# The layout of the products in a banded attention's value stage

## The chip, the core and the metric

The kernel runs on one core of one Trainium2 chip. The metric is the device time of one execution in microseconds (us). The core has five engines that work side by side, each in the order of its own instruction stream: TensorE (PE, with its weight loads as PEld), VectorE (DVE), ScalarE (ACT), GpSimd (POOL) and SyncE (SP, which here only issues transfers). They meet through semaphores.

## What is computed

A sum of two attentions goes through a gated feed-forward part with an RMS norm ahead of it. The local attention sees, for every token, only the seven tokens at distance -3 to 3:

```python
q_d = q.reshape(B, H, Sd, factor, D).mean(axis=3)      # k_d, v_d alike; factor = 4
out_up = np.repeat(sm_attn(q_d, k_d, v_d), factor, axis=2)
mask = np.abs(pos[:, None] - pos[None, :]) < factor
scores = np.where(mask, scale * np.matmul(q, k.transpose(0, 1, 3, 2)), -1000000000.0)
out_local = np.matmul(softmax(scores), v)
x = (out_up + out_local), as rows of 8 heads x 64        # 4608 tokens x 512
xn = x / rms * rms_g
out = (silu(xn @ w_gate) * (xn @ w_val)) @ w_out         # inner width 1536
```

B = 8, H = 8, S = 576, D = 64. Everything is float32; the weights come as float64 bits.

## The kernel before

**Chunks.** The 4608 tokens are worked off in 18 chunks of 256. A chunk is made of two units (`j`) of 128 tokens. In a unit a partition stands for (segment of 36 tokens, batch, head pair), and along the partition lie parity (two heads), 4 tokens and 64 elements.

**The banded attention of a chunk** (class `Attention`) runs in eight steps `i`, one for each unit, parity and pair of tokens (`trio`). Each step has 2 tokens x 7 offsets x 64 elements = 896 numbers per partition:

- `score` (L427) multiplies q by the seven neighbours of k, `score_sum` (L433) adds up 64 elements for each of the 14 scores, both on DVE. Then comes a softmax over seven (L443 to L470).
- `value_scalar` (L480) and `value` (L489) write the seven products of a share and a row of v into a tile `prod`: the first `na` offsets on ACT, one instruction for each token and offset with 64 elements; the last two on POOL, one instruction of 256 elements; what lies between on DVE. `na` is 1 in chunk 0, 2 in chunks 1 and 2, 3 in chunk 3, and 4 from chunk 4 on, so DVE's share is 512, 384, 384, 256 and then 128 elements.
- `value_sum` adds up the seven products. In chunks 0 and 1 (`self.pt` set) PE does it with products by the identity (L504), from chunk 2 on DVE with one reduction (L509).

The tile `prod` has two buffers, which scores and values share: a step's products can only be written when the sum two steps back has read its own.

Behind the eight steps come the sum with the coarse attention (L526), squares on ACT (L532), the norm's mean on PE (L539), an inverse root (L547 and L554 on DVE, then from chunk 2 on three Newton steps on POOL, L564 to L567), the scaling (L571, DVE), the transposes on PE (L582) and the split of x into `xh` (L584, ACT) and `xl` (L588, DVE).

**The feed-forward part of a chunk** (class `Inner`) has 12 tiles `f` of the inner width. Each is 24 products of 256 columns on PE (L658), a tanh on ACT (L664), two DVE operations (L667, L672), a rounded copy `hs` on ACT (L677) and its rest (L680, on POOL in chunks 0 and 1, on DVE after them); two tiles later follow six products of 512 columns (L639). `ps_h`, in which the products of L658 land, has three buffers.

**The order.** In chunk `c` the loop at L1057 puts the attention steps of chunk `c + 1`, and up to four pairs of heads of the coarse attention (L292 to L361), between the tiles `f`, at places given by numbers in `steps` (L592). So the value steps of chunk `c + 1` share DVE and ACT with the feed-forward part of chunk `c`. Chunk 0, with the decoding of the weights, has an order worked out from rough times of instructions (L1019 to L1054). DVE, POOL and SP then keep program order. The coarse attention's sums of four tokens are made by transfers: SP issues a plain load (L279), POOL three that accumulate onto it (L277), each after the one before has landed. POOL has them in the same queue as the products (L489) and the Newton steps.

Of the kernel before, what the change touches and what calls it, by code (L numbers as in the profile page):

```python
# [8 lines left out]
FP32 = mybir.dt.float32  # L9
# [8 lines left out]
DRAM = bass.MemoryType.DRAM  # L18

P = 128  # L20
B, H, S, D = 8, 8, 576, 64
FAC = 4                 # tokens per group of the coarse attention; half-width of the band
SD = S // FAC           # 144 groups
HALF = SD // 2          # 72
NO = 2 * FAC - 1        # 7 diagonals
HALO = FAC - 1
SP = S + 2 * HALO
DM, DF = H * D, 1536
KT = DM // P            # 4 head pairs, also the contraction tiles of the first products
NF = DF // P            # 12  # L30
NPAIR = B // 2
SEG = 36                # tokens of a segment; partition = (segment 16, batch 2, head pair 4)
NSEG = S // SEG
US = 4                  # tokens of every segment in one unit of work
UPP = SEG // US         # units per pair of batches
NU = NPAIR * UPP        # 36 units of 128 tokens
C = 256                 # tokens of a chunk of the feed-forward part
NCH = NU // 2
WPC = 512               # weights decoded at a time, per partition
LAG = 2  # L40
# [52 lines left out]
def attn_moe_kernel(  # L93
# [21 lines left out]
    band = ctx.enter_context(tc.tile_pool(name="band", bufs=2))  # L115
# [13 lines left out]
    class Weight:  # L129
        """A weight's tiles, the last four in places that hold raw weights first."""  # L130

# [24 lines left out]

    # A float64 weight comes as its bits. Its high word, read as a float32, is scaled so that the top
    # of its exponent is float32's (what lies under float32's normal range goes towards zero); moved
    # up by three, and joined by the sign and the top three bits of the low word, it is the weight's
    # float32, which (times the norm's gain) is split exactly into two float32r parts.  # L160
    def load_weight(src, hi_lo, f, n, gain, k):
# [10 lines left out]

        # The sign and the last bits come in one word: the low one, or (signed zeros) the high one.
        def last_bits(engine):
# [63 lines left out]
        def split_on_tensor(pool, tag):  # L238
            # w * gain - hi as products with diagonals, exact but for the rounding of w * gain
            hi, lo = st["hi"], st["lo"]  # L240
            lp = pool.tile([P, *hi.shape[1:]], FP32, name=tag)
            nc.tensor.matmul(out=lp, lhsT=ident_sb if k is None else diag["gain"][:, k], rhs=st["w"], start=True, stop=False)
            nc.tensor.matmul(out=lp, lhsT=diag["minus"], rhs=hi, start=False, stop=True)
            nc.scalar.copy(out=lo, in_=lp)
# [15 lines left out]

# [1 line left out]
    up_dram = {}  # L262
# [23 lines left out]
    class Coarse:  # L286
        """Two heads of the coarse attention."""

# [88 lines left out]

# [1 line left out]
    def load_kv(src, u, par):  # L379
# [7 lines left out]

    def window(t, s0, o0=0, o1=NO):
        b_ = t[:, :, :]
# [11 lines left out]
    class Attention:  # L401
        """The banded attention, the sum with the coarse one, and the norm of one chunk's tokens."""

# [68 lines left out]
        def value_scalar(self, i):  # L472
            j, par, s0 = trio[i]
            if (j, par) not in self.v:
                self.load_value(j, par)
            pr = self.pr[i] = band.tile([P, NO, 2, D], FP32, name="prod")
            p = self.sc[:, j, par, s0:s0 + 2]
            for s in range(2):
                for o in range(self.na):
                    nc.scalar.activation(  # L480
                        out=pr[:, o, s], in_=self.v[j, par][:, s0 + s + o], func=AF.Copy, scale=p[:, s, o:o + 1],
                    )
# [144 lines left out]

# [1 line left out]
    late = []  # L629
# [18 lines left out]
    class Inner:  # L648
        """One tile of the feed-forward part's inner width."""

# [35 lines left out]

# [1 line left out]
    coarse = [(b, hp) for b in range(B) for hp in range(KT)]  # L688
    done = 2 * KT

    # The weights' decoding, the first two chunks' attention and the first chunk's feed-forward part
    # share VectorE, in an order worked out from rough times of the instructions.
    class Clock:
# [32 lines left out]
    finished, decoded, fetched, rank = {}, [], [], {}  # L726
# [28 lines left out]

    # TensorE's clock halves while it idles; products that nobody reads keep it up in the gaps.
    def warm_lane():
# [173 lines left out]
    def raw_loads():  # L931
        # Until they are written, the weights' last places hold raw ones.
        first = [(w, 1, h) for w in wg + wv for h in range(2)]
        second = [(w, i, 0) for w in wo for i in (1, 2)]
        users = {}
        for n, piece in enumerate(pieces):
            if n < place[0, 16]:
                options = [("first", i) for i in range(NF1)] + [("second", i) for i in range(NF2)]
            else:
                options = [("stage", i) for i in range(RAW_BUFS)]  # L940
                options += [("second", i) for i in range(4) if n < (place[1, NF - 4] if i % 2 == 0 else place[1, NF - 2])]

            def slot():
                free = [(finished[users[o]] if o in users else RAW_AT, o) for o in options if users.get(o) in finished or o not in users]
                return min(free) if free else None

            yield lambda: slot() and max(slot()[0], RAW_AT)
            kind, i = o = slot()[1]
            users[o] = "raw done", n
            spot = {"first": first, "second": second, "stage": [None] * RAW_BUFS}[kind][i]  # L950
            load(("raw", n), lambda: piece[0](spot and spot[0].raw_place(*spot[1:])), 1.46)
# [45 lines left out]
    scaled = {n for (t, _), n in place.items() if t == 0}  # L997
# [21 lines left out]
    with tc.manual_schedule(engines={mybir.EngineType.DVE, mybir.EngineType.Pool, mybir.EngineType.SP}):  # L1019
# [3 lines left out]
        group = [sum_loads(0, 0, nc.scalar)]  # L1023
# [33 lines left out]
    for c in range(1, NCH):  # L1057
        todo = []
        if c + 1 < NCH:
# [5 lines left out]
            for i, it in enumerate(coarse[done:done + n]):  # L1065
                at = 0.2 + 5.0 * i / n
# [3 lines left out]
        for f in range(NF):  # L1070
            it = Inner(att, f)
# [3 lines left out]
            while todo and todo[0][0] < f + 1:  # L1075
                step = todo.pop(0)[1]
# [12 lines left out]
def _layouts(i):  # L1089
    import numpy as np  # L1090
    q, k, v = i["q"], i["k"], i["v"]
    a = {}
    a["q_band"] = q.reshape(NPAIR, 2, KT, 2, NSEG, UPP, US, D).transpose(0, 5, 3, 4, 1, 2, 6, 7).reshape(NU, 2, P, -1)
    pad = ((0, 0), (0, 0), (HALO, HALO), (0, 0))
    a["k_pad"], a["v_pad"] = np.pad(k, pad), np.pad(v, pad)
    t = np.stack([q, k], 1).reshape(B, 2, 2, 2, 2, SD, FAC, D)  # batch, q/k, half, head pair, parity, group, j, d
    a["qk_sum"] = t.transpose(0, 6, 4, 7, 2, 1, 3, 5).reshape(B, FAC, P, 2, -1)
# [42 lines left out]
```

## Time and profile before

Three runs took 1214.41, 1214.95 and 1220.25 us; the median is 1214.95.

| | us |
|---|---|
| median of the runs | 1214.95 |
| span of the profiled execution | 1216.1 |
| its own time beside the span | not given by the page |
| DVE, sums of the value stage (L509), 128 | 224.1 |
| ACT, products of the value stage (L480), 1024 | 262.6 |
| POOL, products of the value stage (L489), 144 | 114.2 |
| chunks 12 to 15, from end to end | 54.6 each |
| chunk 17, without any attention beside it | 44.2 |

The span runs from the first to the last instruction. "Busy" is the time in which at least one instruction of the engine was under way. In a row of a group the numbers after the bar are busy time in us, mean duration of one in ns, and the idle time of the engine ahead of them with what ended it ("<-"). A name such as `prod<-sc,kv` says what is written from what. Matmuls are pipelined and their ends are modelled, so a PE without a gap isn't PE at its peak; the granted clock is a share of full speed. Here is the page's picture of the span in 40 slices (busy tenths):

```profile
PE   1894766998999999999999999999999999999998
DVE  5699997699979898888887979798898989898332
ACT  0467643446464747464637464747464654637221
POOL 3467675355131212121212121211112121211000
```

The first seven slices or so are the decoding of the weights and chunk 0, the last three have no attention left.

### The profile page before, as it was taken

How to read it: one execution, taken by the hardware profiler on the slowest of the kernel's cores; microseconds unless marked ns; L12 is line 12 of the kernel's file. 1: busy time of each engine (PE TensorE's matmuls, PEld its weight loads, DVE VectorE, ACT ScalarE, POOL GpSimd, SP SyncE). 2: the span in 40 equal slices, each digit the busy share in tenths (PEclk: the TensorE clock that was granted, in tenths of full speed). 3: DMA queues.
4: the chain of work that ended last, by engine and by line, in shares of the span. 5: the costliest groups of instructions: out<-in, count | busy, mean ns of one | idle time of the engine just before them, and what ended most of it. 6: DMA issues, size and time to landing. Idle time of an engine off the chain costs nothing. (4 is left out here: it accounts for less than half of the span.)

```text
span 1216.1 us, 22187 instructions
## 1 busy us (share of the span) xinstructions
PE 1104.6 (91%) x7944; PEld 1011.3 (83%) x7944; DVE 1012.4 (83%) x1766; ACT 617.1 (51%) x2241; POOL 339.3 (28%) x520
## 2 busy tenths in 40 slices
PE   1894766998999999999999999999999999999998
PEld 1674766988999998989898989899989898989997
DVE  5699997699979898888887979798898989898332
ACT  0467643446464747464637464747464654637221
POOL 3467675355131212121212121211112121211000
PEclk9565788998999999999999999999999999999999
DMA  9946538355536161616161616132222313120000
GB/s 242 227 140 200 194 90 197 96 131 95 139 70 149 34 151 42 150 42 147 41 144 44 148 43 148 43 99 61 72 79 59 85 53 90 48 85 18 1 19 18
DMA packets 77294, 119.57 MB, mean 98 GB/s; under 512 B 27264, under 2 KB 36736, under 8 KB 77184
## 3 DMA queue, kind: packets, MB, share of 16 engines
q1 hardware_dynamic: 47760, 91.12, 25.5%
q0 software_dynamic: 11520, 21.24, 11.4%
q10 hardware_dynamic: 17904, 5.80, 2.1%
q8 instruction: 62, 1.02, 0.4%
q14 instruction: 48, 0.39, 0.1%
HBM read 106.33 MB, written 11.80 MB: 97 GB/s over the span
## 5 line engine op out<-in xcount | busy, mean ns | idle before, releaser
L639 PE MATMUL ps_o<-wo,hs 128*128 128x512 f32 x1296 | 363.4, 401 | 20.7 <-DVE hs L680 18.4
L658 PE MATMUL ps_h<-xh,wg 128*128 128x256 f32 x1728 | 358.6, 286 | 8.6 <-DVE sil L672 8.6
L658 PE MATMUL ps_h<-xh,wv 128*128 128x256 f32 x1728 | 340.5, 279 | 0.0
L658 PEld LDWEIGHTS ps_h<-xh,wg 128*128 128x128 f32 x1728 | 288.9, 193 | 21.1 <-DVE sil L672 11.2
L480 ACT ACTIVATE prod<-kv,sc 128x64 f32<-128x64 f32 x1024 | 262.6, 338 | 50.8 <-DVE x_t L509 35.2
L658 PEld LDWEIGHTS ps_h<-xh,wv 128*128 128x128 f32 x1728 | 281.5, 189 | 3.2 <-issue 0.2
L639 PEld LDWEIGHTS ps_o<-wo,hs 128*128 128x128 f32 x1296 | 221.7, 189 | 58.0 <-DVE hs L680 22.6
L658 PE MATMUL ps_h<-xl,wg 128*128 128x256 f32 x864 | 247.5, 286 | 1.0 <-DVE xl L588 1.0
L658 PE MATMUL ps_h<-xl,wv 128*128 128x256 f32 x864 | 241.7, 280 | 0.0
L509 DVE TENSOR_REDUCE x_t<-prod 128x128 f32<-128x896 f32 x128 | 224.1, 1762 | 6.3 <-PE ps_a L582 3.4
L677 ACT ACTIVATE hs<-sil 128x256 fp32r<-128x256 f32 x216 | 89.8, 416 | 203.5 <-DVE sil L672 170.2
L489 POOL TENSOR_TENSOR prod<-sc,kv 128x256 f32<-128x256 f32 x144 | 114.2, 813 | 272.1 <-DVE x_t L509 116.5
L658 PEld LDWEIGHTS ps_h<-xl,wg 128*128 128x128 f32 x864 | 166.9, 193 | 8.8 <-DVE xl L588 1.2
L658 PEld LDWEIGHTS ps_h<-xl,wv 128*128 128x128 f32 x864 | 163.5, 189 | 1.6
L427 DVE TENSOR_TENSOR prod<-q_t,kv 128x896 f32<-128x896 f32 x140 | 152.4, 1090 | 10.0 <-DMA q_t<-in_q_band_dram 9.7
L664 ACT ACTIVATE sil<-ps_h 128x256 f32<-128x256 f32 x216 | 81.6, 378 | 150.0 <-PE ps_h L658 125.6
L433 DVE TENSOR_REDUCE sc<-prod 128x14 f32<-128x896 f32 x144 | 153.7, 1076 | 0.0
L667 DVE SCALAR_TENSOR_TENSOR sil<-sil,ps_h 128x256 f32<-128x256 f32 x216 | 89.4, 414 | 61.5 <-ACT sil L664 61.5
L680 DVE TENSOR_TENSOR hs<-sil,hs 128x256 fp32r<-128x256 f32 x192 | 80.3, 418 | 32.6 <-ACT hs L677 32.6
L277 POOL DMA_DIRECT2D qk<-in_qk_sum_dram x42 | 38.5, 916 | 190.9 <-DMA qk<-in_qk_sum_dram 172.6
L672 DVE SCALAR_TENSOR_TENSOR sil<-sil,ps_h 128x256 f32<-128x256 f32 x216 | 89.0, 412 | 2.1
L532 ACT ACTIVATE up_t<-x_t 128x128 f32<-128x128 f32 x144 | 44.1, 306 | 45.1 <-DVE x_t L526 43.0
(116 smaller groups left out, 1132.2 us busy)
## 6 DMA issues: line engine op xcount, KB each, us to landing
kv<-in_k_pad_dram SPq DMA_DIRECT2D x72, 320.0 KB
kv<-in_v_pad_dram SPq DMA_DIRECT2D x72, 320.0 KB
qk<-in_qk_sum_dram POOLq DMA_DIRECT2D x42, 288.0 KB, 4.7
out_dram<-o_sb SPq DMA_DIRECT2D x36, 256.0 KB
q_t<-in_q_band_dram SPq DMA_DIRECT2D x70, 128.0 KB
vs<-in_v_sum_dram POOLq DMA_DIRECT2D x42, 144.0 KB, 3.5
wg<-in_w_gate_dram SPq DMA_DIRECT2D x8, 512.0 KB
wg<-in_w_val_dram SPq DMA_DIRECT2D x8, 512.0 KB
```

The costliest lines, as they stand in the source:

```text
L427: engine.tensor_tensor(out=pr[:, :, a:b], in0=bcast(q[:, s0:s0 + 2], 2, b - a), in1=window(k, s0, a, b), op=ALU.mult,)
L433: nc.vector.tensor_reduce(out=self.sc[:, j, par, s0:s0 + 2], in_=self.pr[i], axis=AX.X, op=ALU.add,)
L480: nc.scalar.activation(out=pr[:, o, s], in_=self.v[j, par][:, s0 + s + o], func=AF.Copy, scale=p[:, s, o:o + 1],)
L489: engine.tensor_tensor(out=self.pr[i][:, a:b], in0=bcast(p[:, :, a:b].rearrange("p s o -> p o s"), 3, D), in1=window(self.v[j, par], s0, a ...
L509: nc.vector.tensor_reduce(out=self.x[j][:, s0:s0 + 2, par], in_=pr.rearrange("p o s d -> p s d o"), axis=AX.X, op=ALU.add,)
L639: nc.tensor.matmul(out=o_ps[c][j], lhsT=lhs[:, cols], rhs=rhs(f)[:, 0], start=(f == 0 and i == 0), stop=(f == NF - 1 and i == 2),)
L658: nc.tensor.matmul(out=hp_[:, t], lhsT=wi(f)[:, 0, k], rhs=xi[:, k], start=(n == 0), stop=(n == 3 * KT - 1),)
L664: nc.scalar.activation(out=self.sil, in_=hp_[:, 0], func=AF.Tanh, scale=0.5)
L667: nc.vector.scalar_tensor_tensor(out=self.sil, in0=self.sil, scalar=1.0, in1=self.p[:, 0], op0=ALU.add, op1=ALU.mult,)
L672: nc.vector.scalar_tensor_tensor(out=self.sil, in0=self.sil, scalar=0.5, in1=self.p[:, 1], op0=ALU.mult, op1=ALU.mult,)
L677: nc.scalar.activation(out=self.hh, in_=self.sil, func=AF.Copy)
L680: (nc.gpsimd if self.c in REST_P else nc.vector).tensor_tensor(out=self.hl, in0=self.sil, in1=self.hh, op=ALU.subtract,)
```

## The change

From chunk 2 on, where DVE does the sum, the tile `prod` is allocated in the order (token, element, offset) and not (offset, token, element). A rearranged view gives the rest of the program the axes it had. So the seven products of one output lie next to each other: the reduction reads 896 numbers without a step, where it stepped by 128 numbers (512 bytes), and every product is written with a step of 7 numbers (28 bytes), where it was written densely. That holds for all three writers, ACT (L480), DVE and POOL (L489). Chunks 0 and 1, whose sums PE makes, keep the old layout.

```diff
             if (j, par) not in self.v:
                 self.load_value(j, par)
-            pr = self.pr[i] = band.tile([P, NO, 2, D], FP32, name="prod")
+            pr = band.tile([P, NO, 2, D] if self.pt else [P, 2, D, NO], FP32, name="prod")
+            pr = self.pr[i] = pr if self.pt else pr.rearrange("p s d o -> p o s d")
             p = self.sc[:, j, par, s0:s0 + 2]
...
                 self.x[j][:, s0:s0 + 2, par], in_=pr.rearrange("p o s d -> p s d o"), axis=AX.X, op=ALU.add,
```

(The last line is not changed; it shows the view that the sum reads.) The rest of the diff takes out comments. No instruction is added, removed or moved: on every engine the same instructions stand in the same order and wait for the same engines. Lines behind L476 move down by one in the changed kernel; names with a line number here mean the kernel before, unless said otherwise.

## The prediction

> **What bounds the kernel now.** The first view is the page: its head,
>
> ```profile
> span 1216.1 us, 22187 instructions
> ```
>
> and its busy times (share of the span, instructions):
>
> ```profile
> PE 1104.6 (91%) x7944; PEld 1011.3 (83%) x7944; DVE 1012.4 (83%) x1766; ACT 617.1 (51%) x2241; POOL 339.3 (28%) x520
> ```
>
> TensorE (PE) is the bound on average, VectorE (DVE) next. An average says nothing of a stage, so the second view is the busy time by stretches, cut at ends of chunks over the part in which the changed sums run, 234 to 1122 us. Columns: stretch, length, busy time (instructions) of each engine, granted TensorE clock, DMA share, GB/s.
>
> ```profile
> 234.30:305.40 71.10, 66.09 (x486) 60.52 (x485) 68.72 (x108) 39.95 (x159) 36.08 (x49) 0.93 0.57 123
> 305.40:425.30 119.90, 118.98 (x896) 109.35 (x895) 108.68 (x197) 69.03 (x272) 28.64 (x53) 1.00 0.42 97
> 425.30:790.20 364.90, 351.41 (x2605) 321.27 (x2604) 310.71 (x573) 199.48 (x775) 78.97 (x156) 0.98 0.42 95
> 790.20:847.80 57.60, 57.60 (x436) 52.74 (x436) 52.03 (x96) 33.28 (x130) 8.05 (x20) 1.00 0.26 70
> 847.80:903.40 55.60, 54.54 (x418) 50.75 (x417) 50.76 (x91) 31.29 (x120) 8.59 (x20) 1.00 0.27 73
> 903.40:1121.90 218.50, 206.94 (x1482) 192.10 (x1482) 199.92 (x336) 117.65 (x438) 40.20 (x80) 1.00 0.23 65
> ```
>
> Length less PE's busy time is what PE stands still: 5.0, 0.9, 13.5, 0, 1.1 and 11.6 us, together **32 us**. To this comes what a lower granted clock costs: 7% of 71 us is 5.0 us, 2% of 365 us is 7.3 us. So however much DVE is relieved, some 44 us is the ceiling. The third view is PE's waits, asked for each stretch (us in total, times, longest), here from 234 to 305 us:
>
> ```profile
> PE ps_o L639 <- POOL hs L680: 2.3, 2, 1.8
> PE ps_a L304 <- DVE xl L588: 1.7, 1, 1.7
> PE ps_h L658 <- DVE xl L588: 1.0, 1, 1.0
> ```
>
> from 425 to 790 us:
>
> ```profile
> PE ps_o L639 <- DVE hs L680: 13.5, 8, 2.7
> ```
>
> and from 848 to 1122 us:
>
> ```profile
> PE ps_h L658 <- DVE sil L672: 7.7, 8, 1.7
> PE ps_o L639 <- DVE hs L680: 4.9, 5, 1.1
> ```
>
> Nearly always PE waits for a small DVE instruction. What matters is what stands ahead of that one on DVE, which works in program order. The change leaves the order on every engine as it was, so the rows of the timeline can be walked with new durations.
>
> **The sums (line 509).** From the groups of instructions, shapes kept apart (busy us, mean ns of one, idle before):
>
> ```profile
> L509 DVE TENSOR_REDUCE x_t<-prod 128x128 f32<-128x896 f32 x128 | 224.1, 1762 | 6.3 <-PE ps_a L582 3.4 <-ACT prod L480 2.5 <-issue 0.4
> L433 DVE TENSOR_REDUCE sc<-prod 128x14 f32<-128x896 f32 x144 | 153.7, 1076 | 0.0
> ...
> L452 DVE TENSOR_REDUCE m_b<-sc 128x16 f32<-128x112 f32 x18 | 4.6, 258 | 0.0
> ```
>
> The score sum (L433) reads as many elements, 896, without a step and takes 1076 ns; L509 reads them with a step of 512 bytes and takes 1762. New, it reads runs of seven and gives 128 results. Does a short run cost? L452 reads runs of seven: between it and L433 lie 784 elements and 818 ns, 1.04 ns each, at 16 and 14 results, so a run of seven shows no price. I take **1.08 us**, 0.69 us less; 128 sums make 88 us of DVE. Bounds: 1.08 (no such read is shown faster) and 1.76 (the step was not the cause).
>
> **The writes.** Each product now lands 28 bytes from the last. The writers in the same view, on ACT and on POOL:
>
> ```profile
> L480 ACT ACTIVATE prod<-kv,sc 128x64 f32<-128x64 f32 x1024 | 262.6, 338 | 50.8 <-DVE x_t L509 35.2 <-DVE sc L470 10.8 <-ACT xh L584 3.1
> ```
>
> ```profile
> L489 POOL TENSOR_TENSOR prod<-sc,kv 128x256 f32<-128x256 f32 x144 | 114.2, 813 | 272.1 <-DVE x_t L509 116.5 <-ACT xh L584 96.5 <-DVE m_g L317 27.1
> ```
>
> The nearest that the trace has, an ACT instruction with a dense output and one that writes every second word:
>
> ```profile
> L171 ACT ACTIVATE o_sb<-wg 128x512 f32<-128x512 f32 x24 | 15.9, 662 | 16.7 <-DMA wg<-in_w_gate_dram 7.1 <-DMA wg<-in_w_out_dram 2.7 <-POOL wg L232 2.7
> ```
>
> ```profile
> L179 ACT ACTIVATE wg<-wg 128x512 uint32<-128x512 uint16 x8 | 5.3, 666 | 0.5 <-DMA wg<-in_w_val_dram 0.5
> ```
>
> Of L480's 1024 writes 976 change (8 per sum from chunk 4 on, 4 and 6 in chunks 2 and 3; the first two chunks' 48 don't), and 128 writes each on POOL and DVE. No row shows such a write. From below: L179 writes every second word and takes 666 ns where L171, its output dense, takes 662; so nothing. A gain is excluded: the same elements lay in one run before. From above: the price of L509's step, 686 ns over 896 elements, 0.77 ns each: 0.05 us for an ACT write (64 elements), 0.10 for a DVE one (128), 0.20 for a POOL one (256). The nearest row is L179, so I take nothing for ACT and DVE; for POOL, already at 3.2 ns an element, half the upper end, 0.1 us.
>
> [...]
>
> **From 848 to 1122 us: 12.6 us idle.** Chunk 12's end in the timeline (start, length, [idle before]): PE,
>
> ```profile
> 954.32 0.73 PE L639 MATMUL ps_o<-wo,hs 128*128 128x512 f32 x2 [0.94 <-DVE hs L680]
> ...
> 961.34 0.39 PE L658 MATMUL ps_h<-xh,wg 128*128 128x256 f32 x1 [1.60 <-DVE sil L672]
> ```
>
> DVE,
>
> ```profile
> 939.21 3.48 DVE L509 TENSOR_REDUCE x_t<-prod 128x128 f32<-128x896 f32 x2 [0.53 <-PE ps_a L582]
> ...
> 959.29 1.67 DVE L509 TENSOR_REDUCE x_t<-prod 128x128 f32<-128x896 f32 x1
> 960.87 0.41 DVE L672 SCALAR_TENSOR_TENSOR sil<-sil,ps_h 128x256 f32<-128x256 f32 x1
> ```
>
> and ACT:
>
> ```profile
> 941.09 3.94 ACT L480 ACTIVATE prod<-kv,sc 128x64 f32<-128x64 f32 x16 [0.56 <-ACT xh L584]
> ```
>
> From 939.21 on DVE has no gap, and all eight sums stand ahead of the L672 for which PE waits at 961.34: 8 x 0.69 is 5.5 us. What is late next is ACT: a sum frees one of two product buffers, and the 16 writes of a pair take 3.94 us, now more than the pair's sums (3.48), then far more (2.16), so a part of the 5.5 us goes into DVE waiting for ACT. Walked row by row with 1.08 us, that happens at the sixth and seventh sum, and L672 ends near 957.1 instead of 961.3. PE, by then 1.1 us earlier, wants it at 958.6. Both waits go. With 0.05 us more on each of the 48 writes from 941.09 on it ends near 958.6, still just in time. I take **12 us**.
>
> **From 234 to 305 us: 5.0 us idle, 5.0 us clock.** DVE is busy 68.7 of 71.1 us here. First and last of the six sums ahead of PE's wait for POOL's hs, and that wait:
>
> ```profile
> 235.47 1.76 DVE L509 TENSOR_REDUCE x_t<-prod 128x128 f32<-128x896 f32 x1
> ...
> 249.47 1.78 DVE L509 TENSOR_REDUCE x_t<-prod 128x128 f32<-128x896 f32 x1
> ```
>
> ```profile
> 253.41 0.97 PE L639 MATMUL ps_o<-wo,hs 128*128 128x512 f32 x3 [1.78 <-POOL hs L680]
> ```
>
> POOL's product before that hs needs the buffer that the sixth sum frees: 4.1 us earlier against 1.8 us waited. The two waits for xl come behind nine sums, but also behind POOL's inverse root, whose queue holds DMAs. Of the 10 us I take **6**.
>
> **From 425 to 790 us** the longest total, 13.5 us, has the same look and another cause. Chunk 6 on DVE, POOL and PE:
>
> ```profile
> 582.61 1.29 DVE L571 TENSOR_TENSOR x_t<-x_t,rinv 128x512 f32<-128x512 f32 x2 [7.45 <-POOL rinv L567]
> ```
>
> ```profile
> 579.48 1.52 POOL L489 TENSOR_TENSOR prod<-sc,kv 128x256 f32<-128x256 f32 x2
> ```
>
> ```profile
> 584.30 0.97 PE L639 MATMUL ps_o<-wo,hs 128*128 128x512 f32 x3 [2.10 <-DVE hs L680]
> ```
>
> DVE stands idle 7.45 us for POOL's inverse root (L564 to L567); the hs for which PE waits stands behind L571. POOL's queue has accumulating DMAs ahead of the root, each waiting for the one before. No sum lies on that path, but two strided POOL writes do: 2 x 0.1 us in six chunks costs **1 us**. Only two of the eight waits, 0.6 us each, at 480 and 785 us, come behind sums:
>
> ```profile
> 785.01 0.74 PE L639 MATMUL ps_o<-wo,hs 128*128 128x512 f32 x2 [0.64 <-DVE hs L680]
> ```
>
> They give **1 us**, and the 0.9 us idle from 305 to 425 us another **1 us**.
>
> **Sum.** 12 + 6 + 1 + 1 - 1 = 19 us; 1216.1 - 19 = 1197. The page gives a span and no time around it; this span is 1.15 us above the median of the runs (1214.95), so the time is **1196 us**. Of 88 us taken off DVE about a fifth comes off the kernel, since DVE's slack hides the rest; where that cover is thin, ACT is next.
>
> **Rivals.**
> (1) *More comes free.* DVE ahead by some us also frees SP's load buffers sooner, and with them the DMA chain of 425 to 790 us. SP's waits there (us, times, longest):
>
> ```profile
> SPq L385 <- DVE prod L489: 119.6, 19, 10.5
> ```
>
> ```profile
> SPq L279 <- PE ps_a L343: 13.1, 6, 2.5
> ```
>
> The first row speaks for it, the second against: in each of six chunks the transfer that starts the chain's second half waits for a PE product. Half of the 13.5 + 7.3 us there and 4 us more in 234 to 305: 1196 - 10 - 4 = 1182.
> (2) *Writes pay as reads do.* POOL's 12 x 0.2 us in 425 to 790 is 1.4 us more than summed, with 1 us of clock; from 234 to 305 DVE's larger products (384 and 256 elements) take 0.3 and 0.2 us more, 3.8 us in all, so 4 of the 6 go; the late stretch, without room, loses 4: 1196 + 10 = 1206.
> (3) *Slower: ACT becomes the bound.* By the walk L672 is back at 961.3 from **0.106 us** more per ACT write on (958.6 at 0.05; the last 2.7 us are 48 writes of 0.056). At 0.15 us it is 48 x 0.044 = 2.1 us a chunk worse than before, in 14 chunks 30 us: 1245. Against it: L179. For it: no row has this step.
> (4) *The sum stays slow*, because of its form and not the step: 1216. Against it: L452.
>
> **Chances.** Forecast 0.52; (1) 0.12; (2) 0.18, two thirds of it under 1208.9; (3) 0.11; (4) 0.07. Half a per cent, 6 us, is about what a measurement of this kernel tells from no change. Faster by more: 0.52 + 0.12 + 0.12 = 0.76; within: 0.06 + 0.07 = 0.13; slower: 0.11. The range runs from (1) to (4), 1182 to 1216, and leaves out (3) and the lower half of (1).
>
> **What would show it.** Right: L509 at 1.08 us; 16 writes of L480 still in 3.9 to 4.1 us (4.7 would be (2), over 5.6 (3)); PE idle under 2 us from 848 to 1122; DVE's wait for POOL before L571 still there up to 790 us; new waits of L509 for ACT's products. Wrong: that wait before L571 shrinks together with PE's, POOL's L489 takes over 1.2 us, or L509 stays above 1.3 us.

## The result, and the profile after

The changed kernel took 1181.91 us (median of four runs, 1178.05 to 1182.47), the kernel before, run beside it, 1215.05 (1214.41 to 1220.25). The ratio is 0.971, with a 95% interval of 0.969 to 0.973. That is **33 us faster by the medians and 36 by the ratio** (33 to 38 by its interval), where the prediction had 19. 1181.91 lies 0.09 us under the lower end of its range. The profiled execution took 1178.05 us, 1.75 us more than its span; it was the fastest of the four, so the gains that are read from its profile add up to more, 39.8 us, than the medians differ by.

The page after, first its span and then its busy times:

```profile
span 1176.3 us, 22187 instructions
...
PE 1089.8 (93%) x7944; PEld 999.5 (85%) x7944; DVE 935.8 (80%) x1766; ACT 612.9 (52%) x2241; POOL 345.5 (29%) x520
```

DVE gives up 77 us, the span 40. The groups of instructions (busy us, mean ns of one, idle before). Lines are now one further down, so the sum is L510, ACT's product L481, POOL's and DVE's L490:

```profile
L481 ACT ACTIVATE prod<-kv,sc 128x64 f32<-128x64 f32 x1024 | 270.4, 407 | 12.6 <-DVE sc L470 10.6 <-DVE x_t L510 0.9 <-PE ps_a L505 0.7
...
L510 DVE TENSOR_REDUCE x_t<-prod 128x128 f32<-128x896 f32 x128 | 136.4, 1076 | 18.7 <-ACT prod L481 13.6 <-PE ps_a L583 3.5 <-POOL prod L490 1.4
L490 POOL TENSOR_TENSOR prod<-sc,kv 128x256 f32<-128x256 f32 x144 | 122.6, 885 | 214.6 <-DVE x_t L510 64.8 <-ACT xh L585 61.9 <-ACT hs L678 51.8
...
L490 DVE TENSOR_TENSOR prod<-sc,kv 128x128 f32<-128x128 f32 x112 | 46.3, 449 | 1.0
```

The sum takes 1076 ns, what the score sum took before. ACT waited 35.2 us for the sums before (in its row of the prediction), now 0.9; in exchange the sums wait 13.6 us for ACT, before 2.5. The products are longer: POOL's 885 ns (813), ACT's 407 (338), DVE's 449 (323). DVE's row in the same view of before:

```profile
L489 DVE TENSOR_TENSOR prod<-sc,kv 128x128 f32<-128x128 f32 x112 | 34.4, 323 | 1.0
```

The stretches, cut at the same ends of chunks as in the prediction (length, busy and instructions of each engine, granted clock, DMA share, GB/s):

```profile
233.20:299.00 65.80, 64.13 (x503) 58.34 (x502) 62.53 (x108) 39.99 (x159) 34.90 (x49) 1.00 0.61 133
299.00:413.50 114.50, 114.50 (x863) 105.51 (x862) 99.95 (x198) 68.56 (x272) 28.47 (x52) 1.00 0.43 101
413.50:765.20 351.70, 344.67 (x2606) 315.02 (x2606) 281.99 (x573) 198.70 (x776) 81.67 (x156) 1.00 0.42 99
765.20:822.40 57.20, 57.20 (x437) 52.66 (x435) 47.58 (x96) 33.62 (x131) 8.46 (x20) 1.00 0.26 70
822.40:877.10 54.70, 54.70 (x421) 51.11 (x420) 47.29 (x92) 31.65 (x120) 9.39 (x20) 1.00 0.27 74
877.10:1080.90 203.80, 203.80 (x1483) 191.51 (x1482) 178.98 (x335) 114.50 (x437) 42.51 (x80) 1.00 0.25 70
```

The two kernels by stage, from these rows and those of before. "Still" is the length less PE's busy time, "clock" what the granted clock costs (to 0.1 us, from the trace's records of the clock):

| stage | before: length, still, clock | after | gain | predicted |
|---|---|---|---|---|
| chunk 0, to 234 us | 234.3 | 233.2 | 1.1 | 0 |
| chunks 1 to 3 | 191.0, 5.9, 5.1 | 180.3, 1.7, 0 | 10.7 | 7 |
| chunks 4 to 9 | 364.9, 13.5, 6.8 | 351.7, 7.0, 0 | **13.2** | **0** |
| chunk 10 | 57.6 | 57.2 | 0.4 | 0 |
| chunks 11 to 15 | 274.1, 12.6, 0 | 258.5, 0, 0 | 15.6 | 12 |
| the rest | 94.2 | 95.4 | -1.2 | 0 |

The largest miss stands out: chunks 4 to 9, where nothing was to happen. PE's waits in that stretch (us, times, longest) went from 13.5 to

```profile
PE ps_o L640 <- DVE hs L681: 7.0, 6, 1.7
```

The late chunks are as the prediction walked them. DVE, chunk 12 (start, length, [idle before]):

```profile
911.98 2.08 DVE L510 TENSOR_REDUCE x_t<-prod 128x128 f32<-128x896 f32 x2 [0.53 <-PE ps_a L583]
...
924.18 1.08 DVE L510 TENSOR_REDUCE x_t<-prod 128x128 f32<-128x896 f32 x1 [0.24 <-ACT prod L481]
```

and ACT:

```profile
913.17 4.01 ACT L481 ACTIVATE prod<-kv,sc 128x64 f32<-128x64 f32 x16
...
917.31 3.98 ACT L481 ACTIVATE prod<-kv,sc 128x64 f32<-128x64 f32 x16
```

Sixteen ACT products take 3.98 to 4.01 us where they took 3.94 in the prediction's row. Over all 31 unbroken rows of sixteen the mean is 4.00 us, and 3.98 before. The row of the group gives 69 ns more for each product, but the next one starts before the last ends, 239 ns (median) behind its start in both kernels; what the strided write adds to one instruction lies almost wholly under the next. The row of the group alone would have told the opposite of the timeline.

### The profile page after: what moved, and what is told of

The parts are those of the page before. It is cut to its first block, busy times and chain, and to the rows that moved or that the text cites. A ratio compares the mean times of both kernels' runs of the same rounds, so it can differ in the third digit from the quotient of the medians.

```text
span 1176.3 us, 22187 instructions
## 1 busy us (share of the span) xinstructions
PE 1089.8 (93%) x7944; PEld 999.5 (85%) x7944; DVE 935.8 (80%) x1766; ACT 612.9 (52%) x2241; POOL 345.5 (29%) x520
## 5 line engine op out<-in xcount | busy, mean ns | idle before, releaser
L659 PE MATMUL ps_h<-xh,wg 128*128 128x256 f32 x1728 | 352.3, 283 | 0.0
L659 PE MATMUL ps_h<-xh,wv 128*128 128x256 f32 x1728 | 339.2, 279 | 0.0
L659 PEld LDWEIGHTS ps_h<-xh,wg 128*128 128x128 f32 x1728 | 284.4, 190 | 10.2 <-issue 0.6
L659 PEld LDWEIGHTS ps_h<-xh,wv 128*128 128x128 f32 x1728 | 280.2, 188 | 3.2 <-issue 0.2
L481 ACT ACTIVATE prod<-kv,sc 128x64 f32<-128x64 f32 x1024 | 270.4, 407 | 12.6 <-DVE sc L470 10.6
L659 PE MATMUL ps_h<-xl,wg 128*128 128x256 f32 x864 | 245.1, 284 | 0.4 <-DVE xl L589 0.4
L659 PE MATMUL ps_h<-xl,wv 128*128 128x256 f32 x864 | 241.0, 279 | 0.0
L490 POOL TENSOR_TENSOR prod<-sc,kv 128x256 f32<-128x256 f32 x144 | 122.6, 885 | 214.6 <-DVE x_t L510 64.8
L659 PEld LDWEIGHTS ps_h<-xl,wg 128*128 128x128 f32 x864 | 164.2, 190 | 8.5 <-issue 1.7
L659 PEld LDWEIGHTS ps_h<-xl,wv 128*128 128x128 f32 x864 | 162.8, 188 | 1.6
L427 DVE TENSOR_TENSOR prod<-q_t,kv 128x896 f32<-128x896 f32 x140 | 151.3, 1083 | 10.3 <-DMA q_t<-in_q_band_dram 10.0
L433 DVE TENSOR_REDUCE sc<-prod 128x14 f32<-128x896 f32 x144 | 153.8, 1075 | 0.0
L510 DVE TENSOR_REDUCE x_t<-prod 128x128 f32<-128x896 f32 x128 | 136.4, 1076 | 18.7 <-ACT prod L481 13.6
L277 POOL DMA_DIRECT2D qk<-in_qk_sum_dram x42 | 38.5, 916 | 213.6 <-DMA qk<-in_qk_sum_dram 148.5
L490 DVE TENSOR_TENSOR prod<-sc,kv 128x128 f32<-128x128 f32 (+3 forms) x144 | 74.0, 544 | 1.1
```

The costliest lines, as they stand in the source:

```text
L427: engine.tensor_tensor(out=pr[:, :, a:b], in0=bcast(q[:, s0:s0 + 2], 2, b - a), in1=window(k, s0, a, b), op=ALU.mult,)
L433: nc.vector.tensor_reduce(out=self.sc[:, j, par, s0:s0 + 2], in_=self.pr[i], axis=AX.X, op=ALU.add,)
L481: nc.scalar.activation(out=pr[:, o, s], in_=self.v[j, par][:, s0 + s + o], func=AF.Copy, scale=p[:, s, o:o + 1],)
L490: engine.tensor_tensor(out=self.pr[i][:, a:b], in0=bcast(p[:, :, a:b].rearrange("p s o -> p o s"), 3, D), in1=window(self.v[j, par], s0, a ...
L510: nc.vector.tensor_reduce(out=self.x[j][:, s0:s0 + 2, par], in_=pr.rearrange("p o s d -> p s d o"), axis=AX.X, op=ALU.add,)
L659: nc.tensor.matmul(out=hp_[:, t], lhsT=wi(f)[:, 0, k], rhs=xi[:, k], start=(n == 0), stop=(n == 3 * KT - 1),)
```

## The experiments

The **theory** after the result: the strided writes cost nothing on the path; the sums' time comes back in three separate stages; and in chunks 4 to 9, too, it is the sums that shorten the wait for the chain of `vs` transfers and POOL's inverse root. The **rivals**: the writes cost something that the sums pay for; the gain of 425 to 790 us comes from elsewhere (an earlier stage, chance). Each ratio below is that of the kernel against the one before, run on the same chip in the same session, with its 95% interval; the changed kernel's is 0.9707 (0.9687 to 0.9727). The stages that the text compares are in rows of the view by stretches, cut at ends of chunks.

### The read alone, and the write alone

e1: the products are written densely, as before, and the sum reads 896 numbers in a row in groups of seven. e2: the products are written with the step of 28 bytes, and the sum reads with a step of 512 bytes. In both, the sum of an output takes in products of other outputs.

```diff
 e1, against the kernel before
-in_=pr.rearrange("p o s d -> p s d o")
+in_=pr.rearrange("p o s d -> p (o s d)").rearrange("p (s d o) -> p s d o", s=2, o=NO)
 e2, against the changed kernel: the tile stays [P, 2, D, NO], its numbers are read as if it were [P, NO, 2, D]
-in_=pr.rearrange("p o s d -> p s d o")
+in_=self.flat[i].rearrange("p (o s d) -> p s d o", s=2, o=NO)
```

> The sum reads 896 numbers without a step, the writes stay dense as before (so the seven numbers that are added are not the seven products of one output). Theory A, all of the gain is the sum's 0.69 us and the strided writes cost next to nothing on the path: as the changed kernel or up to 3 us faster, 1179 to 1182 us. Rival B, the strided writes (DVE 0.13 us, POOL 0.07 us each, ACT's longer records) give back a part on the path: 1177 us or less. L509 at 1.08 us in both.

> The writes have the 28-byte step, the sum still reads with a step of 512 bytes (over other numbers than the products of one output). Theory A: DVE is busy some 17 us longer (112 x 0.13 and the larger ones), on the path that is 1 us a chunk in the chunks that DVE bounds and some of it in the first, 1219 to 1226 us. Rival: the writes are free on the path, 1212 to 1217 us.

e1: 1185.46 us, ratio 0.972 (0.968 to 0.976), which takes in the changed kernel's. e2: 1222.06, ratio 1.002 (1.000 to 1.005), at most 6 us slower, which is too near to no change to part theory and rival. The sum in e1:

```profile
L509 DVE TENSOR_REDUCE x_t<-prod 128x128 f32<-128x896 f32 x128 | 136.8, 1078 | 25.1 <-ACT prod L480 13.6 <-POOL prod L489 6.8 <-PE ps_a L582 3.8
```

The groups of e2:

```profile
L482 ACT ACTIVATE prod<-kv,sc 128x64 f32<-128x64 f32 x1024 | 272.7, 405 | 52.3 <-DVE x_t L511 37.6 <-DVE sc L470 10.8 <-ACT xh L586 3.1
L511 DVE TENSOR_REDUCE x_t<-prod 128x128 f32<-128x896 f32 x128 | 225.4, 1771 | 6.2 <-PE ps_a L584 3.7 <-ACT prod L482 2.4
```

The write alone makes the products longer as in the changed kernel (ACT's 405 ns), and the sum stays at 1771; the read alone brings the whole gain. What the step of 28 bytes costs is off the path, as far as these intervals tell: in the changed kernel DVE's product of 128 elements takes 126 ns more, 1 ns an element, POOL's 72 ns more for 256.

### One stage at a time

e3, e4 and e5 take the new layout for the values of chunks 5 to 11, 12 to 17 and 2 to 4 alone (a chunk's values run in the stage of the chunk before):

```diff
-pr = band.tile([P, NO, 2, D] if self.pt else [P, 2, D, NO], FP32, name="prod")
+dense = self.pt or not 5 <= self.c <= 11        # e4: 12 to 17; e5: 2 to 4
+pr = band.tile([P, NO, 2, D] if dense else [P, 2, D, NO], FP32, name="prod")
```

> The new layout for the values of chunks 5 to 11 alone, which run beside chunks 4 to 10, the stretch from 425 to 848 us in which the prediction saw no gain. Theory A, the sums ahead move loads and shorten the wait for POOL's root there, and the clock then stays up: 13 to 14 us, 1201 to 1202 us, with PE idle about 7 us in the stretch and a granted clock of 1.00. Rival, the gain there comes from the chunks before it or differs from run to run: 1208 us or more.

> The new layout for the values of chunks 12 to 17 alone, beside chunks 11 to 16. Theory A: the waits of 848 to 1122 us go and nothing else does, 13 to 15 us, 1200 to 1202 us, with PE idle under 1 us there. Rival, the late chunks are fast only because the earlier ones ran ahead: under 10 us, 1205 us or more.

> The new layout for the values of chunks 2 to 4 alone, beside chunks 1 to 3. Theory A: 9 to 11 us from 234 to 425 us, half of it granted clock, 1204 to 1206 us. Rival, these chunks' gain needs the later ones: 1210 us or more.

| | time, us | ratio | gain at 1215 us |
|---|---|---|---|
| e3, middle | 1205.14 | 0.989 (0.985 to 0.993) | 13.4 |
| e4, late | 1201.21 | 0.985 (0.982 to 0.989) | 17.9 |
| e5, early | 1211.93 | 0.996 (0.994 to 0.999) | 4.5 |
| sum | | | 35.8 |
| all | 1181.91 | 0.971 (0.969 to 0.973) | 35.6 |

The three add up to the whole, within their intervals. The middle and the late part act in their own stages alone; here the stretches of e3,

```profile
423.40:775.50 352.10, 344.68 (x2607) 315.02 (x2606) 281.99 (x573) 198.63 (x775) 81.61 (x156) 1.00 0.42 99
834.50:1108.60 274.10, 261.29 (x1898) 242.66 (x1898) 250.70 (x425) 148.96 (x556) 48.71 (x100) 1.00 0.23 67
```

and of e4:

```profile
423.30:790.70 367.40, 351.94 (x2601) 320.67 (x2600) 311.06 (x573) 199.02 (x775) 78.67 (x156) 0.98 0.41 95
846.70:1105.20 258.50, 258.50 (x1902) 242.62 (x1901) 226.22 (x426) 146.08 (x556) 51.80 (x100) 1.00 0.25 71
```

e3 has the middle of the changed kernel (352.1 us, PE busy 344.7) and the late stage of the one before (274.1), e4 the reverse. So the 13 us of the middle are made there, by the sums of the middle, and the early stage hands nothing on. The early part alone gained less than expected, 4.5 us for 9 to 11, which meets the rival's mark (1210 us or more). If its gain needed the later chunks, though, the three would fall short of the whole, and they don't. In e5's profile chunks 1 to 3 took 183.3 us against 191.0, but that execution took 1208.07 us where the median is 1211.93. The late part gained 17.9, more than the 13 to 15 expected.

### POOL's chain in the middle

Is it still the inverse root that ends the waits of chunks 4 to 9? e6 and e11 leave out the last of three Newton steps for chunks 5 to 10 (in the kernel before and in the changed one), e7 and e8 add two and three small POOL instructions, which multiply by one, to the last step of these chunks. e12 does the inverse root of every chunk on VectorE.

```diff
 e6 on the kernel before, e11 on the changed one
-            for _ in range(3):
+            for _ in range(2 if 5 <= self.c <= 10 else 3):
 e7 (2) and e8 (3), in the last step, ahead of rinv
+                    for _ in range(2 if 5 <= self.c <= 10 and step == 2 else 0):
+                        nc.gpsimd.tensor_scalar(out=t, in0=t, scalar1=1.0, scalar2=0.0, op0=ALU.mult, op1=ALU.add)
 e12
-NEWTON = (0,1)
+NEWTON = tuple(range(18))
```

> The kernel before with two steps of POOL's inverse root and not three for chunks 5 to 10 (so the norm there is a little less exact): POOL's chain ahead of L571 is four instructions, 1.1 us, shorter and the sums are as before. Theory A, the waits from 425 to 790 us follow that chain and cost granted clock when they last 2 us: idle falls by about 1.1 us in each of six chunks (6 to 7 us) and the clock by 0.98 to 1.00 gives 6 to 7 us more, 1202 to 1203 us. Rival, no clock in it: 1208 to 1209 us. Rival, the sums set these waits: 1215 us.

> The changed kernel with two more small POOL instructions (a product by one) in the last step of the inverse root of chunks 5 to 10, some 0.6 us. Theory A: the six waits of 0.7 to 1.7 us grow by 0.6 us each, 3.5 us, and the longest of them, now over 2 us, cost clock: 4 to 8 us over the changed kernel, 1186 to 1190 us. Rival, the waits are no longer on the path: 1182 us.

> As the one before with three small instructions, 0.9 us. Theory A: 5.2 us of idle and, with waits of 1.6 to 2.6 us, clock in four or more of six chunks, 1.2 us each: 10 to 13 us over the changed kernel, 1192 to 1195 us. Rival, idle alone: 5 us, 1187 us.

> The changed kernel with two steps instead of three in POOL's inverse root of chunks 5 to 10 (the last step is left out). Theory (after the change the chain from the first vs transfer over POOL's root to L572 still sets the idle time of TensorE in chunks 4 to 9, 7.0 us): the chain gets 1.0 to 1.2 us shorter each time, the idle time goes to 0 to 2 us, and the whole gets 5 to 7 us faster than the changed kernel, 1175 to 1177. Rival (another wait ends there as late): within 2 us of 1181.9.

> The changed kernel with the inverse root of every chunk on VectorE (nine to twelve small instructions of 128x8 a chunk) instead of POOL; the rest of the order is rearranged by that. Theory (VectorE now has the room, as it idles beside TensorE, and POOL's queue with its vs transfers no longer stands before L572): TensorE's idle time in chunks 4 to 9 goes from 7.0 us to 0 to 2, time 1174 to 1178. Rival (the 1 us more of VectorE a chunk takes back what the sums gave, or products that come late through the new order cost more): 1181 to 1190.

| | time, us | ratio | chunks 4 to 9: length, PE busy |
|---|---|---|---|
| e6, step less, before | 1210.38 | 0.9935 (0.991 to 0.996) | 356.9, 347.4 |
| e7, two more, changed | 1190.95 | 0.977 (0.973 to 0.981) | 360.6, 349.1 |
| e8, three more, changed | 1192.80 | 0.979 (0.976 to 0.982) | 359.3, 349.4 |
| e11, step less, changed | 1176.56 | 0.9675 (0.964 to 0.971) | 346.8, 344.7 |
| e12, on VectorE, changed | 1172.98 | 0.9645 (0.962 to 0.967) | 342.6, 342.6 |

The middle of e6 by stretches:

```profile
425.70:782.60 356.90, 347.40 (x2607) 316.68 (x2607) 310.75 (x573) 198.80 (x776) 74.11 (x132) 1.00 0.43 97
```

that of e11:

```profile
415.40:762.20 346.80, 344.66 (x2607) 315.08 (x2606) 281.95 (x573) 198.81 (x776) 76.69 (x132) 1.00 0.43 100
```

and that of e12:

```profile
417.40:760.00 342.60, 342.60 (x2605) 315.18 (x2604) 290.61 (x627) 200.46 (x775) 66.86 (x84) 1.00 0.43 102
```

With the old sums a shorter root gives 8 us (e6); with the new ones a longer root takes 8 to 10 (e7, e8), a shorter one gives 4 to 5 (e11), and without it on POOL the waits are gone (e12). So the chain set the end of these waits before, as the prediction said, and sets it after. e6 gained less than the 12 to 13 us expected: in its profile the idle time went from 13.5 to 9.5 us, the loss by the clock from 6.8 to 1.7. Yet the new sums shortened these waits, with POOL's root as it was. If the chain sets them, the sums must shorten the chain; the next section measures it. e12, 9 us under the changed kernel by the medians of two sessions, is the fastest kernel of the study (8 us by the ratios).

### What in the chain got shorter

The chain's first link is the load that starts the sum of v, put out by SP; three accumulating transfers on POOL and the rest of the root follow. Chunk 6 before, POOL (DMA issues among its instructions):

```profile
571.46 0.86 POOL L277 DMA_DIRECT2D vs<-in_v_sum_dram  x1 [5.44 <-DMA vs<-in_v_sum_dram]
575.12 0.84 POOL L277 DMA_DIRECT2D vs<-in_v_sum_dram  x1 [2.81 <-DMA vs<-in_v_sum_dram]
...
578.71 0.90 POOL L277 DMA_DIRECT2D vs<-in_v_sum_dram  x1 [1.37 <-DMA vs<-in_v_sum_dram]
```

and SP:

```profile
566.30 0.34 SPq L279 DMA_DIRECT2D vs<-in_v_sum_dram  x1
567.91 0.55 SPq L385 DMA_DIRECT2D kv<-in_v_pad_dram  x1
568.55 0.54 SPq L411 DMA_DIRECT2D q_t<-in_q_band_dram  x1
```

DVE's last score product ahead of them:

```profile
566.79 1.09 DVE L427 TENSOR_TENSOR prod<-q_t,kv 128x896 f32<-128x896 f32 x1
```

The same place after, POOL,

```profile
555.22 0.86 POOL L277 DMA_DIRECT2D vs<-in_v_sum_dram  x1 [3.29 <-DMA vs<-in_v_sum_dram]
559.32 0.84 POOL L277 DMA_DIRECT2D vs<-in_v_sum_dram  x1 [3.24 <-DMA vs<-in_v_sum_dram]
...
562.99 0.89 POOL L277 DMA_DIRECT2D vs<-in_v_sum_dram  x1 [1.45 <-DMA vs<-in_v_sum_dram]
```

SP,

```profile
551.47 0.33 SPq L279 DMA_DIRECT2D vs<-in_v_sum_dram  x1
551.90 0.55 SPq L385 DMA_DIRECT2D kv<-in_v_pad_dram  x1
552.55 1.31 SPq L411 DMA_DIRECT2D q_t<-in_q_band_dram  x1
```

DVE,

```profile
549.81 1.08 DVE L427 TENSOR_TENSOR prod<-q_t,kv 128x896 f32<-128x896 f32 x1
...
566.89 1.29 DVE L572 TENSOR_TENSOR x_t<-x_t,rinv 128x512 f32<-128x512 f32 x2 [6.47 <-POOL rinv L568]
```

and PE:

```profile
568.57 1.19 PE L640 MATMUL ps_o<-wo,hs 128*128 128x512 f32 x4 [1.20 <-DVE hs L681]
```

The wait is the chain's length and nothing else. PE stops 15.9 us behind SP's load, before (584.30 - 2.10 - 566.30, PE's row from the prediction) and after (568.57 - 1.20 - 551.47), and starts again 1.7 us behind the start of L571. The traces give the same 15.9 and 1.7 us in all six chunks of both kernels. So what PE waits is the time from SP's load to L571 less 14.2 us.

From SP's load to the third of POOL's transfers it is 578.71 - 566.30 = 12.4 us before and 562.99 - 551.47 = 11.5 after; from there to L571 it is 3.9 us in both (582.61 and 566.89). Over the six chunks the first part has a mean of 12.4 and 11.5, the second of 3.9 and 3.9, and L571 comes 16.3 and 15.4 us behind SP's load. So the root and POOL's products take what they took; the **transfers** go out sooner. Of their three steps only the first is shorter: from SP's plain load to POOL's first transfer it is 4.1 us before and 3.2 after (means of six), to the second 4.65 and 4.62, to the third 3.62 and 3.65. POOL stands idle ahead of that first transfer each time (0.9 to 5.4 us before, 1.7 to 3.3 after). So it is SP's plain load that lands sooner, 2.6 us behind its issue by the trace's semaphores, and 3.5 before (means of six).

What else changed beside it is the load of kv and q_t. It needs a buffer that DVE's last score product (L427) frees. Before, DVE was late: L427 ended at 567.88, the kv load went out at 567.91 (0.02 to 0.03 us behind L427's end in all six chunks), the two loads 1.6 and 2.3 us behind the first `vs` transfer. After, it is done at 550.89, and the kv load goes out directly behind the `vs` load (0.4 us). Over all profiles of this study, the kernels with old sums in the middle put the kv load out 1.2 to 2.6 us behind, and the third of POOL's transfers goes out 12.4 us (mean of 30, standard error 0.1) behind SP's; those with new sums at 0.4 us, and 11.8 (63, 0.1). That goes with the theory that the place of the loads does it, but it parts nothing: with them goes all else that a faster DVE does.

So three kernels hold the buffer back in the changed kernel, by one more small DVE instruction behind the last score sum that also reads the kv buffer (e9), and their twins have the instruction without that read (e10). e13 and e14 repeat the two with a wider tile for its result, e15 and e16 without a tile of its own.

```diff
 e9, behind score_sum(i); e13 the same with a tile [P, 16]; e10 and e14 with in0=self.sc[:, j, par, 3, 1:2]
+if i == 7 and 5 <= self.c <= 10:
+    hold = band.tile([P, 1], FP32, name="hold", bufs=1)
+    nc.vector.tensor_tensor(out=hold, in0=self.qk[j, par][1][:, 0, 0:1], in1=self.sc[:, j, par, 3, 0:1], op=ALU.mult)
 e15: out and in0 are the kv buffer's first column, which is not read again; e16: the first column of self.pr[i]
```

> The changed kernel, and in chunks 4 to 9 one more instruction on VectorE (a product of two single columns, behind the last sum of scores) that reads the last kv buffer of the scores, so that this buffer comes free later, as it did before the change. Theory (the loads that go out directly behind the first vs transfer are what makes the vs transfers land sooner): kv and q_t go out 2 to 3 us behind the first vs transfer instead of directly behind it, the time from the first vs transfer to the third that POOL adds goes from 11.5 us to 12.2 to 12.6, TensorE's idle time in chunks 4 to 9 from 7.0 us to 11 to 14, and the whole is 5 to 9 us slower than the changed kernel's 1181.9. Rival (the vs transfers land sooner for another reason, or chance): 11.5 us stays, and the time is within 2 us of the changed kernel and of e10.

> As e9, but the added VectorE instruction reads only the scores, so no buffer is held longer. Both theories: kv and q_t go out directly behind the first vs transfer, 11.5 us to the third added vs transfer, within 2 us of the changed kernel's 1181.9.

> e9 once more, with its one added column in a tile of 64 bytes a partition instead of 4; nothing else differs, the order of every engine is the same. If it is the 4 bytes, by which every tile behind it in the SBUF moved, that made e9 slow (its matmuls of chunks 11 to 15 take 282 ns instead of 279 and 396 instead of 394, and these chunks 262.7 us without idle time, against 258.5), then chunks 11 to 15 take 258.5 us again and the whole 1176 to 1182. If it is the added instruction or the order, 262.7 stays and 1190 to 1196. The place of the kv load: if a kv load 4 us behind the first vs transfer is no worse than one directly behind it, the third added vs transfer goes out at 10.8 to 11.3 us as in e9, and TensorE idles 2 to 5 us in chunks 4 to 9; if that was chance, 11.6 to 11.9 and 6 to 8 us.

> e10 once more, with the 64-byte tile. If it is the 4 bytes: chunks 11 to 15 in 258.5 us, the whole within 3 us of the changed kernel's 1181.9. If it is the added instruction: 262.7 us and 1190 to 1196. The kv load goes out directly behind the first vs transfer: third added vs transfer at 11.5 to 11.9 us, and 1 to 4 us slower than e13 if the place of the kv load matters, equal if not.

> e9 and e13 once more, but the added instruction writes into the kv buffer that it reads (its first column is not needed any more), so that there is no tile more; the order of every engine is that of e13. If it is the added tile (all tiles behind it lie 4 or 64 bytes further), whose matmuls follow each other at 117 and 120 ns in place of 114, chunks 11 to 15 take 258.5 us again and the whole 1175 to 1180, since e9 and e13 idle only 2.5 and 3.6 us in chunks 4 to 9. If it is the added instruction or the order, 262 to 264 us stay and 1190 to 1198.

> e10 and e14 once more without a tile more: the added instruction works in the products' buffer, whose sum has been taken, and kv comes free as in the changed kernel. If it is the added tile: chunks 11 to 15 in 258.5 us, the whole 1179 to 1185. A kv load 4 us later (e15) against directly behind (here): third added vs transfer at 10.4 to 11.5 us there, at 11.5 to 12.0 here, and e15 faster by 1 to 5 us, if the place of the load decides; equal if not.

| | time, us | ratio | kv behind first `vs`, us | third `vs`, us | PE still, chunks 4 to 9 | chunks 11 to 15 |
|---|---|---|---|---|---|---|
| changed | 1181.91 | 0.9707 (0.969 to 0.973) | 0.4 | 11.5 | 7.0 | 258.5 |
| e9, held, 4-byte tile | 1193.25 | 0.9805 (0.977 to 0.984) | 4.1 | 11.1 | 2.5 | 262.8 |
| e10, twin | 1193.99 | 0.9806 (0.978 to 0.984) | 0.4 | 11.7 | 4.7 | 262.8 |
| e13, held, 64-byte tile | 1198.14 | 0.9845 (0.982 to 0.987) | 4.1 | 11.4 | 3.6 | 263.9 |
| e14, twin | 1200.20 | 0.9857 (0.983 to 0.988) | 0.4 | 12.1 | 5.9 | 263.9 |
| e15, held, no tile | 1186.07 | 0.9741 (0.971 to 0.977) | 4.1 | 12.6 | 10.6 | 258.5 |
| e16, twin | 1180.78 | 0.9706 (0.968 to 0.973) | 0.4 | 11.5 | 5.2 | 258.5 |

(In the held kernels the load is late in five of the six chunks; the means of the transfers are over all six.)

e9, e10, e13 and e14 missed what was expected of their time and are spoilt as measurements of it: they lose 11 to 18 us, most of it for another reason, told below. It also makes PE come later to its wait, 16.3 to 16.4 us behind SP's load in place of 15.9, so their idle times can't be held against the others'. e15 and e16 are free of it. e15's middle,

```profile
416.40:773.30 356.90, 346.33 (x2607) 316.43 (x2606) 282.06 (x578) 198.57 (x776) 81.72 (x156) 1.00 0.42 97
```

and e16's:

```profile
416.70:766.60 349.90, 344.67 (x2607) 315.00 (x2606) 282.12 (x578) 198.89 (x776) 82.31 (x156) 1.00 0.42 99
```

With the buffer freed later the transfers take 12.6 us in place of 11.5, PE stands still 5.4 us more, the middle is 7.0 us longer and the kernel 5.3 us slower by the medians, a ratio 0.0035 higher. That is the direction of the theory as it stood for e9, and against what was written for e15 after e9 and e13. For in those two, with the same late load, the transfers took 11.1 and 11.4 us, 0.6 less than in their twins. One pair speaks for the theory and two against it, so that the place of the kv load moves the chain is not shown.

The traces show one more thing that differs. Ahead of SP's load for v, POOL puts out the last accumulating transfer of the sums of q and k (`qk`, L277). In e15 it goes out 0.5 to 1.6 us ahead of SP's load in the five chunks with a late kv load, in e9 and e13 from 0.6 ahead to 0.5 behind, and the third `vs` transfer goes out at 12.7 to 13.3 us in e15 and at 10.4 to 12.0 in e9 and e13. So e15 and e16 differ in more than the kv load (there `qk` lies 0.5 us ahead on the mean, in e15 1.1). No run sets the place of `qk` alone. Nor was a kv load 1.6 us late, as before, made by itself.

## Why the prediction was half right

**The sum: right.** 1.08 us was forecast, 1076 ns measured: in runs of seven the sum takes what the score sum takes in runs of 64 (1076 before, 1075 after). e1 has the whole gain with the read alone: rival (4) is out.

**The writes: right on the path, wrong per instruction.** Forecast were nothing for ACT and DVE and 0.1 us for POOL, the upper ends 0.05, 0.10 and 0.20. POOL's took 0.07 more. DVE's took 0.13 more, above its upper end. ACT's single instruction took 0.07 more, above its upper end too, but 16 in a row only 0.02 us (means of the 31 rows), about 1 ns each, and that is what the walk needed. The 1 us that POOL's strided writes were to cost in 425 to 790 us is not there: from the third transfer to L571 it is 3.9 us as before. e2 bounds all three at 6 us if the sums are slow; with fast sums e1 and the changed kernel differ by less than their intervals. Rivals (2) and (3) are out as times: L481's sixteen stayed at 4.0 us (4.7 and 5.6 were their marks). DVE's writes did cost more than (2) had for them, without effect on the time that can be told.

**848 to 1122 us: right, a little small.** Forecast 12, measured 15.6 in chunks 11 to 15 less 1.2 given back behind them, and no wait is left. The 12.6 us of idle time were not all: PE's busy time fell too, 261.5 to 258.5 us; why is not shown. The new waits of the sums for ACT came as foreseen (13.6 us over the whole kernel), and PE doesn't wait for them in these chunks.

**234 to 425 us: right, too small in this profile.** Forecast 7, measured 10.7; the profiles with the new sums in this stage lie at 180.3 to 186.0 us, those with the old ones at 189.3 to 192.5. e5 alone gives 4.5 (1.7 to 7.4).

**425 to 790 us: wrong, and here lies the miss.** The step reads: "No sum lies on that path", with 1 us gained and 1 us lost. The wait for POOL's root in front of L571 was rightly named, and it is still there (6.47 us). But the path was followed back only to POOL's queue, and the transfers in it were taken to last as long as before. They don't: from SP's load to the third of POOL's transfers it is 12.4 us before and 11.5 after, and PE's wait is that path's length less a constant. So the sums do act on it. How they do is open. The account that e9 to e16 were to test is: sums, DVE's last score product, the buffer, SP's loads of kv and q_t, the `vs` load beside them; its last link is not shown, as the pairs e9 to e16 contradict each other.

Rival (1) had this account and priced it at 10 us here; it got 0.12, since "the transfer that starts the chain's second half waits for a PE product". That row is true, and says nothing about how long the transfers after it take. That the rival's 1182 us meets the measured 1181.91 is in part luck: it took the late chunks at 12 us, which gave more, and the time a constant 1.15 us under the span, of which below.

The gain is 13.2 us in the profile, 13.4 alone (e3): 6.5 us of standing still, and 6.8 us of clock, which the prediction saw in the same rows (7.3 us), put into the ceiling and then into no term of its sum. A mean of 0.9 us on each of six waits was enough to bring all of them under 1.9 us (2.66 at the longest before, 1.72 after), and in the changed kernel none was followed by a lower clock; in e6 the clock still cost 1.7 us of 6.8.

**The time beside the span.** The prediction kept the median 1.15 us under the profile's span, as it was before. After, the profiled execution took 1.75 us more than its span, and the median lies 3.9 us above that execution. So the 39.8 us that the stages gain in the profile are 33 between the medians.

## What to carry to other kernels

Where an engine waits for a transfer, the length of the transfer is not a given: here the same load of SP landed 3.5 us behind its issue before and 2.6 after. Ask which other transfers go out beside it, who frees their buffers, and whether the change moves that; that these set the length was not shown here. Put a price on the clock for the waits that get shorter, not only on the wait itself: of the 13.2 us in chunks 4 to 9, 6.8 were clock, 1.7 us behind each of four waits of 2.10 to 2.66 us. And read what a strided write costs from a row of such instructions back to back, not from the mean of one: on ACT it was 69 ns by the mean and about 1 ns by the row.

## What the runs showed of the hardware

**A tile more, and slower matmuls.** A tile of 4 bytes a partition that only chunks 4 to 9 use makes chunks 11 to 15 of e10 4.3 us longer (262.8 for 258.5), without idle time. Its matmuls between 900 and 1000 us (count, busy us, mean ns):

```profile
L659 PE MATMUL ps_h<-xh,wv 128*128 128x256 f32 x185 | 37.7, 281 | 0.0
...
L659 PE MATMUL ps_h<-xl,wg 128*128 128x256 f32 x95 | 26.8, 282 | 0.0
```

and those of the changed kernel:

```profile
L659 PE MATMUL ps_h<-xh,wv 128*128 128x256 f32 x191 | 38.1, 279 | 0.0
...
L659 PE MATMUL ps_h<-xl,wg 128*128 128x256 f32 x94 | 26.1, 278 | 0.0
```

In chunks 11 to 15 it is 117 ns (median) from one start of L659 to the next instead of 114, and 120 with the 64-byte tile (e13 and e14). e15 and e16 have the same instruction without the tile, e15 with the order of e13 on every engine, and are back at 114 ns and 258.5 us. So it is the tile and not the instruction or the order; that the tiles behind it moved, as e13 and e15 put it, no run shows. By the medians it is worth 7 us (e9 against e15) to 19 (e14 against e16), as much as most of the edits tried here.

**The clock after a short wait.** Before, chunk 5, after a wait of 2.52 us (the view by stretches, 4 us each; the clock is the third number from the end):

```profile
520.00:524.00 4.00, 1.49 (x8) 0.92 (x7) 2.38 (x5) 0.11 (x1) 1.01 (x5) 1.00 0.35 92
524.00:528.00 4.00, 4.00 (x22) 3.89 (x21) 3.62 (x5) 2.59 (x8) 0.62 (x1) 0.57 0.00 0
```

4 us at 0.57 lose 1.7 us. From 230 to 1075 us in the 18 profiles of this study, 23 of 30 waits of PE of 1.9 us and more were followed within 8 us by such a loss, and 8 of 67 waits of 1.2 to 1.9 us. In the changed kernel the longest wait is 1.72 us, and none was followed by one. In the kernel before alone it was 4 of 4 (2.10 to 2.66 us, 1.7 us lost behind each) and 2 of 7: a wait of 1.74 us at 290.9 us was followed by a loss, one of 1.75 us at 1070.6 was not. So the length alone does not decide it, and the count is no rule.

**The step of a read and of a write.** 896 numbers at a step of 512 bytes cost DVE 0.77 ns each more to read (the sum's 1762 ns before, 1076 after); 128 numbers at a step of 28 bytes cost it 1 ns each more to write (the product's 449 ns after, 323 before).
